# Whole-pair key loads in a cached-attention decode kernel, with three gathers on ScalarE and GpSimd and a later TensorE branch

## The chip, the core and the metric

The kernel runs on one core of a Trainium2 chip. The core has TensorE (matrix products; "PE" in the profile, with its weight loads as "PEld"), VectorE ("DVE"), ScalarE ("ACT"), GpSimd ("POOL") and SyncE ("SP"). Here SyncE only issues transfers, which run on the core's 16 DMA engines. The metric is the time of one execution in microseconds on the device, as the median of several runs.

## The reference

One token (`x` is 1x1x512) goes through a layer norm, attention over a cache of 16384 positions (8 key/value heads of width 128, four query heads on each) and a small mixer MLP. Cut to what matters:

```python
q = (ln(x) @ wq).reshape(1, 1, 32, 128)           # 32 query heads
p = softmax(q @ k.T * 128 ** -0.5)                # k_cache, v_cache: 8 x 16384 x 128, bf16
h = x + (p @ v).reshape(1, 1, 4096) @ wo          # wo: 4096 x 512
u = ln(h)
x1 = u + ...                                      # one position: the padded, shifted h is cut to zeros
out = h + x1 + gelu(ln(x1) @ w3) @ w4             # w3: 512 x 1792, w4: 1792 x 512
```

The token mixer shifts along a sequence of length one, so its shifted parts are zero and `w1`, `w2` are never read. What is read is 79 MB: the keys and values are 33.6 MB each, and `wq`, `wo`, `w3`, `w4` make the rest.

## The kernel before

The eight key/value heads are done as four pairs (`j` = 0 to 3). One pair's keys are 8 MB and its values are 8 MB. Each of the 128 partitions holds a contiguous run of 64 KB of either: `kb` takes a pair's keys (as two halves, `kb[0]` and `kb[1]`), `vb` a pair's values, and `kt` half a pair's transposed keys.

A small planner (`Program`) records every operation with the tiles it reads and writes, works out which operations must wait for which, and writes out each engine's program in the order of recording. An engine works its list strictly in order, so an operation that waits holds everything behind it on that engine. TensorE's part of the four pairs is written once as a loop over registers (`_tensor`), so the sequence of signals from VectorE must be alike in every pair. The operation with no function (`pe(None, ...)`, `dve(None)`) marks a place where a branch is put that never leads away, with a hint for the instruction fetch.

For each pair:

- VectorE transposes the keys (`transpose_keys`, L616) into `kt`, in doubles of two pieces (128x2048 words of 32 bits, two head positions in a word) or in single pieces (128x1024). A half is eight pieces. Pairs 0 to 2 use four doubles in each half; pair 3 uses two singles and three doubles in half 0 and eight singles in half 1.
- TensorE clears a score bank (L627) and adds four products per piece (L633), as soon as the piece is there. A piece of `kt` may be overwritten once TensorE has read it.
- When a half's transposes are done, SyncE issues the load of the next pair's same half (`load_keys(j + 1, y)`), 4 MB. Only the first pair is loaded as one transfer of 8 MB.
- The softmax runs on VectorE (L643 to L651), ScalarE (the exponential, L655) and VectorE again (L659). Meanwhile TensorE runs a spin of 14 passes of two products that nobody reads (L498).
- TensorE multiplies with the values (L670) once GpSimd has told that they have landed (L475) and `pt` is there. Then SyncE issues the next pair's values, since `vb` is free.
- `gather(j)`: VectorE adds four blocks of the result with a factor for each row (L687, L690, the tile `od`), TensorE sums over rows (L694), and VectorE scales and masks into `o_m` (L696).

Behind the pairs, `wo` is multiplied (L739, weights into the place of the keys' first half), then a layer norm, `w3` (L759), the gelu on ScalarE (L769, `hg`, two halves), its transposes on VectorE (L773, `hcol`), and `w4`: the first seven blocks as wide products (L782), copied out by VectorE into `osum` (L785), summed over rows by TensorE (L788), and the last seven blocks as 28 narrow products (L794). Two copies to `fin` (L799, L801) and the output's transfer (L802) end it. TensorE's branch stands between L782 and L788 and waits for the second half of `hcol`.

SyncE's list of transfers, all on one queue and in this order: `wq`, keys 0 (whole), values 0, keys 1 in halves, values 1, keys 2 in halves, values 2, keys 3 in halves, values 3, `wo` in two parts (behind half 0 of pair 3), `w3` and `w4` in three parts (behind half 1 of pair 3), the output.

Of the kernel before, what the change touches and what calls it, by code (L numbers as in the profile page):

```python
# [24 lines left out]
class Program:  # L25
# [150 lines left out]
    def _tensor(self):  # L176
# [51 lines left out]
        for o in loop:  # L228
            ds = [d for d in o.deps if d.own]
            assert not ds or o.at[0] == "value"  # L230
            assert not any(d.dma for d in o.deps)
            for d in ds:
                told.setdefault(o.at[1:3], set()).add((d.sem, d.val - d.worth + 1, d.val))
# [4 lines left out]
        assert v0 > 0 and first - step * last > 0  # L238

        r, rl, ry, rq, rk = (eng.alloc_register(n) for n in ("seen", "landed", "half", "query", "piece"))  # L240
        self.turn, self.turned = rk, KP * pieces
# [123 lines left out]
KP = 8 * DH  # L365
# [5 lines left out]
def bass_sequential_preLN__gqa_block_cached__mixer_s_mlp__decode_kernel(  # L371
# [13 lines left out]
    with ExitStack() as ctx:  # L385
# [60 lines left out]
        kb_all = sb("kb", [128, 256 * DH], BF16)  # L446
# [80 lines left out]
        def variance(i):  # L527
# [7 lines left out]
            for n in range(1 + i):  # L535
# [9 lines left out]
        load("k", kb_all[:, :], pair_rows(A_k_cache, 0), ("r", 0, 0),  # L545
             also=[("r", y, i) for y in range(2) for i in range(RPARTS) if y or i])
# [65 lines left out]
        def transpose_keys(y, cuts):  # L612
            for t, n in zip(cuts, [b - a for a, b in zip(cuts, [*cuts[1:], 8])]):
                view = lambda x, t=t, n=n: x[:, :].bitcast(I32).rearrange("p (x l w) -> p x (l w)", x=2, l=64)[
                    :, :, t * 512:(t + n) * 512]
                P.op("DVE", lambda e, view=view: e.transpose(view(kt), view(kb[y])),  # L616
                     r=[("r", y, i) for i in range(RPARTS)], w=[("kt", t + i) for i in range(n)], worth=n)

        def key_piece(at, n):
            part = kt[:, :].rearrange("p (x f) -> p x f", x=2)[:, :, bass.ds(at, KP)]  # L620
            return part.rearrange("p x (l b s e) -> p b e x l s", l=8, b=2, s=32, e=2)[:, n // 2, n % 2, :, :, :]
# [40 lines left out]
        def values(j):  # L662
            tiles = vb[:, :].rearrange("p (x c l d) -> p x l c d", x=4, c=8, l=8)
            for x in range(VP):
                P.part("value", j, x)
                for it in range(16 // VP):
                    for ct in range(4):
# [4 lines left out]
                            tiles[:, l // 8, l % 8, 4 * ch:4 * ch + 4, :], start=(l < 2), stop=(l >= 30)),  # L672
# [8 lines left out]
        def gather(j):  # L681

            O, key = O_ps[0], ("O", 0)
            for c in range(4):
                block = O[:, c * 128:(c + 1) * 128]
                if c == 0:
                    dve(lambda e, block=block: e.tensor_scalar(od[:, :], block, rowc[:, 0:1], None, ALU.mult),  # L687
                        r=[key, "rowc"], w=["od"], bank=[key])
                else:
                    dve(lambda e, block=block, c=c: e.scalar_tensor_tensor(  # L690
                        od[:, :], block, rowc[:, c:c + 1], od[:, :], ALU.mult, ALU.add),
                        r=[key, "rowc", "od"], w=["od"], bank=[key])
# [3 lines left out]
            dve(lambda e: e.scalar_tensor_tensor(  # L696
                o_m[32 * j:32 * j + 32, :, :], A_ps[0:32, 0:128].rearrange("p (d r) -> p d r", d=4), den[:, 0:1],
                maskdd[0:32, :].unsqueeze(2).to_broadcast([32, 4, 32]), ALU.mult, ALU.mult),
                r=["A", "den", "maskdd"], w=["o_m"], bank=["A"])
# [136 lines left out]
```

## Time and profile before

| what | us |
|---|---|
| median of three runs | 189.87 (189.81 to 189.93) |
| the profiled execution | 189.89 |
| its span, first to last instruction | 188.4 |

| engine | busy us | share of the span |
|---|---|---|
| PE | 137.8 | 73% |
| DVE | 115.8 | 61% |
| ACT | 9.3 | 5% |
| POOL | 5.9 | 3% |
| DMA engines (16, mean) | | 97.9% |

A row of a timeline has the start and the length of a group of instructions, the engine, the line of the kernel, the operation, the tile written and the tiles read, and how many there are; brackets hold the idle time before it and what ended it. A row of the chain of waits has start, length and what the time went to; for a transfer that is the time from its issue to its landing. A row by lines has the busy time, the mean of one in nanoseconds, and the idle time before. A row of transfers ends with the time from issue to landing.

### The profile page before, as it was taken

What the parts mean: (1) busy time and instruction counts of PE and PEld (TensorE: products, weight loads), DVE (VectorE), ACT (ScalarE), POOL (GpSimd) and SP (SyncE); (2) the same over time, 40 slices, a digit from 0 to 9 for tenths busy, and PEclk for the clock granted to TensorE, in tenths of its full rate; (3) what the DMA queues carried; (4) which work ended last, traced back from release to release, by engine and by line L of the source; (5) the groups of instructions that cost most, each with busy time, mean ns of one, the idle gap of its engine ahead of it and who ended that gap; (6) DMA issues with size and microseconds to landing.
All of it is one profiled execution on the core that took longest, in us unless ns stands there. A gap on an engine that the chain in (4) does not pass through costs nothing.

```text
span 188.4 us, 2532 instructions
## 1 busy us (share of the span) xinstructions
PE 137.8 (73%) x820; PEld 59.3 (31%) x824; DVE 115.8 (61%) x141; ACT 9.3 (5%) x16; POOL 5.9 (3%) x11
## 2 busy tenths in 40 slices
PE   1009700599989639998990999999319999886874
PEld 1004200234434413443450344345103433432332
DVE  4900741999645299994508999551449897513154
ACT  3000000000020000000200000020000000500011
POOL 1900000000000000000000000000000000000010
PEclk9999985569999975999998599999955999999998
DMA  6999999999799998999999999997999998899994
GB/s 223 445 445 445 445 445 445 445 445 445 334 445 445 445 543 362 417 389 403 445 445 445 445 445 445 445 445 334 445 445 445 556 403 362 362 440 450 397 411 183
DMA packets 2605, 79.19 MB, mean 420 GB/s; under 512 B 298, under 2 KB 300, under 8 KB 812
## 3 DMA queue, kind: packets, MB, share of 16 engines
q1 hardware_dynamic: 2596, 79.17, 97.9%
q8 instruction: 1, 0.02, 0.0%
q10 hardware_dynamic: 8, 0.00, 0.0%
HBM read 79.17 MB, written 0.00 MB: 420 GB/s over the span
## 4 chain that ended last, share of the span: by engine, by line
DMA 45%; PE 36%; DVE 16%; issue 2%; ACT 0%; SPq 0%; DVEq 0%
DMA kb<-in_A_k_cache_dram 32%; PE banks L633 22%; DMA kb<-in_B_w_dram 13%; DVE kt L616 12%; PE banks L498 6%; PE banks L670 4%; DVE mx L643 1%; PE banks L627 1%; DVE od L690 1%; PE banks L647 1%; PE banks L759 1%; PE banks L694 0%; DVE od L687 0%; DVE osum L785 0%; PE banks L782 0%
## 5 line engine op out<-in xcount | busy, mean ns | idle before, releaser
L616 DVE STREAM_TRANSPOSE kt<-kb 128x2048 int32<-128x2048 int32 (+1 forms) x37 | 71.0, 1985 | 10.4 <-DMA kb<-in_A_k_cache_dram 10.4
L633 PE MATMUL banks<-kt,qn 128*128 x256 | 69.1, 426 | 0.1
L633 PEld LDWEIGHTS banks<-kt,qn 128*128 x256 | 26.8, 105 | 41.0 <-issue 21.5
L498 PE MATMUL banks<-xn 128*128 128x512 bf16 x126 | 28.6, 381 | 0.0
L627 PE MATMUL banks<-qn 128*128 128x512 bf16 x8 | 3.9, 490 | 23.9 <-DVE kt L616 23.9
L498 PEld LDWEIGHTS banks<-xn 128*128 128x128 bf16 x130 | 12.7, 99 | 15.8 <-issue 2.4
L593 PE MATMUL banks<-vb,xn 128*128 x32 | 8.5, 432 | 9.7 <-DVE xn L584 9.7
L670 PE MATMUL banks<-vb,pt 128*32 128x512 bf16 x256 | 14.7, 379 | 0.7 <-POOLq L475 0.7
L659 DVE STREAM_TRANSPOSE pt<-p_sb 64x1024 bf16<-64x1024 bf16 x8 | 9.9, 1239 | 5.4 <-ACT p_sb L655 5.3
L655 ACT ACTIVATE p_sb<-banks,bias 128x1024 bf16<-128x1024 f32 x4 | 4.5, 1114 | 155.4 <-DVE nmh L651 155.4
L670 PEld LDWEIGHTS banks<-vb,pt 128*32 128x32 bf16 x256 | 8.7, 97 | 4.7 <-POOLq L475 0.8
L687 DVE TENSOR_SCALAR od<-banks,rowc 128x128 f32<-128x128 f32 x4 | 1.4, 351 | 14.2 <-PE banks L670 14.2
L643 DVE TENSOR_REDUCE mx<-banks 128x1 f32<-128x1024 f32 x4 | 4.9, 1224 | 8.1 <-PE banks L633 8.1
L627 PEld LDWEIGHTS banks<-qn 128*128 128x128 bf16 x8 | 0.8, 100 | 25.8 <-issue 25.4
L600 DVE STREAM_TRANSPOSE qcol<-banks 64x1024 f32<-64x1024 f32 x4 | 4.8, 1226 | 6.6 <-PE banks L593 6.6
L593 PEld LDWEIGHTS banks<-vb,xn 128*128 128x128 bf16 x32 | 3.5, 108 | 14.3 <-issue 11.6
L539 POOL TENSOR_TENSOR st<-st,expo 128x1 f32<-128x1 f32 (+1 forms) x2 | 1.3, 630 | 175.4 <-DVE st L537 175.4
L506 PE MATMUL banks<-mean 128*128 128x512 f32 (+1 forms) x12 | 6.5, 622 | 0.0
L694 PE MATMUL banks<-od,zo 128*32 128x128 f32 x8 | 1.6, 285 | 6.5 <-DVE od L690 6.5
L680 DVE RECIPROCAL den<-banks 32x1 f32<-32x1 f32 x4 | 0.6, 155 | 7.8 <-PE banks L678 7.8
L690 DVE SCALAR_TENSOR_TENSOR od<-banks,rowc,od 128x128 f32<-128x128 f32 x12 | 4.2, 351 | 0.4
L647 PE MATMUL banks<-mxd,mean 128*128 128x128 f32 x8 | 2.0, 326 | 2.4 <-DVE mxd L644 2.4
(81 smaller groups left out, 49.5 us busy)
## 6 DMA issues: line engine op xcount, KB each, us to landing
kb<-in_A_k_cache_dram SPq DMA_DIRECT2D x6, 4096.0 KB, 24.9
vb<-in_A_wq_dram SPq DMA_DIRECT2D x1, 4096.0 KB, 12.3
kb<-in_A_wo_dram SPq DMA_DIRECT2D x1, 3584.0 KB, 28.5
kb<-in_B_w_dram SPq DMA_DIRECT2D x1, 1792.0 KB, 24.2
kb<-in_B_w_dram SPq DMA_DIRECT2D x1, 896.0 KB, 26.0
kb<-in_B_w_dram SPq DMA_DIRECT2D x1, 640.0 KB, 27.1
kb<-in_A_wo_dram SPq DMA_DIRECT2D x1, 512.0 KB, 29.4
kb<-in_B_w_dram SPq DMA_DIRECT2D x1, 256.0 KB, 27.2
```

The source lines that it names most:

```text
L498: P.unread = lambda e: e.matmul(banks[:, 7, :], copies(xn[:, 0:1], 128), copies(xn[:, 0:1], 512), start=True, stop=True)
L506: pe(lambda e: e.matmul(banks[:, 7, 0:n], mean4[:, :], copies(mean4[:, 0:1], n), start=True, stop=True), r=["mean4"], w=["spare1"])
L593: pe(lambda e, k=k: e.matmul(row[:, bass.ds(P.b, 512)], copies(xn[:, k:k + 1], 128), wq_k[:, k, bass.ds(P.c, REP * DH)], start=(k == 0), s ...
L600: dve(lambda e, g=g, b=b, half=half: e.transpose(qcol[64 * g:64 * g + 64, 2 * b:2 * b + 2, :, :].rearrange("p e m u -> p (e m u)"), half.r ...
L616: P.op("DVE", lambda e, view=view: e.transpose(view(kt), view(kb[y])), r=[("r", y, i) for i in range(RPARTS)], w=[("kt", t + i) for i in r ...
L627: pe(lambda e: e.matmul(row[:, bass.ds(P.y, 512)], copies(none, 128), copies(none, 512), start=True, stop=False, skip_group_check=True), r ...
L633: pe(lambda e, n=n: e.matmul(row[:, bass.ds(P.y, 512)], qn[:, n, bass.ds(P.q, 128)], key_piece(P.k, n), start=False, stop=(n == 3), skip_g ...
L643: dve(lambda e: e.tensor_reduce(mx[:, :], s_all, AX.X, ALU.max), r=[("s", 0), ("s", 1)], w=["mx"], **both)
L655: act(lambda e: e.activation(p_sb[:, :], s_all, ACTF.Exp, bias=bias[:, 0:1], scale=float(SCALE), accum_out=acc[:, :]), r=[("s", 0), ("s", ...
L659: dve(lambda e, g=g: e.transpose(pt[64 * g:64 * g + 64, :, :, g, :], p_sb[64 * g:64 * g + 64, :]), r=["p"], w=["pt"])
L670: pe(lambda e, l=l, ct=ct, ch=ch: e.matmul(O_ps[0][32 * ct:32 * ct + 32, :], pt[:, l, ch, :, :].rearrange("p g u -> p (g u)"), tiles[:, l ...
L690: dve(lambda e, block=block, c=c: e.scalar_tensor_tensor(od[:, :], block, rowc[:, c:c + 1], od[:, :], ALU.mult, ALU.add), r=[key, "rowc", ...
```

## The change

Six things change.

1. Keys of pairs 1 and 2 are loaded as one transfer of 8 MB each. To let such a load start before the last transposes of the pair before it, the keys lie at shifting places in a longer `kb`: pair 0 four pieces up, pair 1 two pieces up, pairs 2 and 3 at the start. The last two pieces of pairs 0 and 1 then lie beyond what the next load writes. Pair 3 is still loaded in halves.
2. A piece of `kt` is contiguous (`KP` is 16 runs of 128 instead of two times 8), and the values are indexed to match.
3. Half 1 of every pair is transposed in eight single pieces.
4. The gathers of pairs 0 to 2 go to ScalarE (four scaled copies into `osum`, later the scaling into `o_m`) and GpSimd (two additions, later the mask). TensorE waits for GpSimd's signal. The gather of pair 3 stays on VectorE, with a GpSimd instruction that passes the signal on.
5. The spin of 14 passes is counted against VectorE's signals and grows from pair to pair, to 14 in the last.
6. TensorE's branch in the tail, and the 28 narrow products, wait for a ScalarE copy of the whole `hcol` (128x448) into `hg` instead of for `hcol` itself.

```diff
@@ _tensor: signals of the gather, and the spin
+            gs = [d for d in o.deps if d.own == "g"]
...
-                self._spin(eng, at[a])
+                passes, body = self.spins.get(id(at[a]), (0, 0))
+                if passes:
+                    by = step // 3
+                    assert now > by * passes
+                    eng.reg_mov(self.turn, now - by * passes)
+                    eng.br("pe_turn")
+                    nc.switch_bb("pe_turn", parent=None)
+                    for _ in range(body):
+                        self.unread(eng)
+                    eng.reg_add(self.turn, self.turn, by)
+                    eng.br_lt(self.turn, r, "pe_turn", "pe_turned")
...
+                if any(d.own == "g" for d in at[a].deps):
+                    eng.wait_ge(self.gathered, rl)
@@ sizes
-KP = 8 * DH
+KP = 16 * DH
+BASE = (4 * KP, 2 * KP, 0, 0)
...
-        kb_all = sb("kb", [128, 256 * DH], BF16)
+        kb_all = sb("kb", [128, BASE[0] + 256 * DH], BF16)
@@ loads of the keys
-        def load_keys(j, y):
+        def load_keys(j, y=None):
             n = 128 * DH
-            load(f"k{y}", kb[y][:, :], pair_rows(A_k_cache, j)[:, y * n:(y + 1) * n], ("r", y, 0),
-                 also=[("r", y, i) for i in range(1, RPARTS)])
+            if y is None:
+                load("k", kb_all[:, BASE[j]:BASE[j] + 2 * n], pair_rows(A_k_cache, j), ("r", 0, 0),
+                     also=[("r", y, i) for y in range(2) for i in range(RPARTS) if y or i] + [("tail", j)])
+            else:
+                load(f"k{y}", kb[y][:, :], pair_rows(A_k_cache, j)[:, y * n:(y + 1) * n], ("r", y, 0),
+                     also=[("r", y, i) for i in range(1, RPARTS)])
@@ transposes
+        def transpose_keys(j, y, cuts):
             for t, n in zip(cuts, [b - a for a, b in zip(cuts, [*cuts[1:], 8])]):
+                at = BASE[j] + (8 * y + t) * KP
+                apart = BASE[j] and y and t >= 6
+                P.op("DVE", lambda e, t=t, n=n, at=at: e.transpose(
+                    kt[:, t * KP:(t + n) * KP].bitcast(I32), kb_all[:, at:at + n * KP].bitcast(I32)),
+                     r=[("tail", j)] if apart else [("r", y, i) for i in range(RPARTS)],
+                     w=[("kt", t + i) for i in range(n)], worth=n)
@@ gather
+            if j < PAIRS - 1:
+                for c in range(4):
+                    act(lambda e, c=c: e.activation(osum[:, c * 128:(c + 1) * 128], O[:, c * 128:(c + 1) * 128],
+                                                    ACTF.Identity, scale=rowc[:, c:c + 1]),
+                        r=[key, "rowc"], w=[("osum", c)], bank=[key])
+                pool(lambda e: e.tensor_tensor(osum[:, 0:256], osum[:, 0:256], osum[:, 256:512], ALU.add),
+                     r=[("osum", c) for c in range(4)] + [("o_m", j - 1)], w=[("osum", 0), ("osum", 1)])
+                P.op("POOL", lambda e: e.tensor_tensor(od[:, :], osum[:, 0:128], osum[:, 128:256], ALU.add),
+                     r=[("osum", 0), ("osum", 1)], w=["od", "gathered"], own="g")
+            else:
...
+                P.op("POOL", lambda e: e.nop(), r=["od"], w=["gathered"], own="g")
             unread(1)
             pe(lambda e: e.matmul(A_ps[0:32, 0:128], zo[:, :], od[:, :], start=True, stop=True),
-               r=["od", "zo"], w=["A"], bank=["A"])
+               r=["gathered"], also=["od", "zo"], w=["A"], bank=["A"])
+            if j < PAIRS - 1:
+                act(lambda e: e.activation(to.rearrange("p d r -> p (d r)"), A_ps[0:32, 0:128], ACTF.Identity,
+                                           scale=den[:, 0:1]), r=["A", "den"], w=[("o_m", j)], bank=["A"])
+                pool(lambda e: e.tensor_tensor(
+                    to, to, maskdd[32 * j:32 * j + 32, :].unsqueeze(2).to_broadcast([32, 4, 32]), ALU.mult),
+                    r=[("o_m", j), "maskdd"], w=[("o_m", j)])
@@ the loop over the pairs
-                transpose_keys(y, (0, 2, 4, 6) if j < PAIRS - 1 else range(8) if y else (0, 1, 2, 4, 6))
+                transpose_keys(j, y, range(8) if y else (0, 2, 4, 6) if j < PAIRS - 1 else (0, 1, 2, 4, 6))
                 scores(j, y)
-                if j < PAIRS - 1:
+                if j == PAIRS - 2:
                     load_keys(j + 1, y)
+                elif j < PAIRS - 2 and y:
+                    load_keys(j + 1)
@@ the tail
-        pe(None, r=[("hcol", 1)])
+        act(lambda e: e.activation(hg[:, :], hcol[:, :, :].rearrange("p m u -> p (m u)"), ACTF.Identity),
+            r=[("hcol", 1)], w=["late", ("hg", 0), ("hg", 1)])
+        pe(None, r=["late"])
...
-                   r=[("hcol", 2 * m // NHC), ("r", 1, len(W3) + piece(W4, m))], w=["n"], bank=["mn"])
+                   r=["late", ("r", 1, len(W3) + piece(W4, m))], w=["n"], bank=["mn"])
```

More of the change, by code (lines that the diff above doesn't have):

```diff
@@ L228, in _tensor @@
         for o in loop:
-            ds = [d for d in o.deps if d.own]
+            ds = [d for d in o.deps if d.own == "v"]
+            gs = [d for d in o.deps if d.own == "g"]
             assert not ds or o.at[0] == "value"
+            assert not gs or o.at[0] in ("rest", "value")
             assert not any(d.dma for d in o.deps)
+            for d in gs:
+                assert d.val == o.at[1] + (o.at[0] == "rest")
+                self.gathered = d.sem
             for d in ds:
@@ L237, in _tensor @@
             assert lo_v <= v0 + parts * j + x <= hi_v
-        assert v0 > 0 and first - step * last > 0
+        assert v0 == 1 and first - step * last > 0
         r, rl, ry, rq, rk = (eng.alloc_register(n) for n in ("seen", "landed", "half", "query", "piece"))
-        self.turn, self.turned = rk, KP * pieces
+        self.turn, self.turned = rk, None
         hint = eng.mark_branch_hint_location()
```

50 lines of the change are left out of this document (24 added, 26 removed).

## The prediction

> **What bounds the kernel now.** I read the page first, then the chain of waits, then SyncE's timeline beside the times from issue to landing. From the page, the span, the DMA row of the 40 slices and the queues:
>
> ```profile
> span 188.4 us, 2532 instructions
> DMA  6999999999799998999999999997999998899994
> q1 hardware_dynamic: 2596, 79.17, 97.9%
> ```
>
> The 16 DMA engines work 97.9% of the span, and every slice but the first and the last reads 7 or more. From the chain of waits (start, length, what):
>
> ```profile
> 1.19 31.19 DMA kb<-in_A_k_cache_dram
> ...
> 119.03 29.68 DMA kb<-in_A_k_cache_dram
> ...
> 157.94 24.21 DMA kb<-in_B_w_dram
> ...
> 185.12 0.70 DVE osum L785
> ...
> 185.87 0.42 PE banks L788 x8
> ```
>
> The chain names compute in the middle, but its DMA pieces are times from issue to landing, most of which a transfer stands in line. Whether the line ever empties is seen from SyncE's timeline (start, length of the issue), and from the DMA view of short windows around single issues, in the order values 0, second key half of pair 1, values 1, second key half of pair 2, values 2, values 3 (last column: us from issue to landing):
>
> ```profile
> 22.43 0.33 SPq L463 DMA_DIRECT2D vb<-in_A_v_cache_dram  x1
> 41.44 9.05 SPq L463 DMA_DIRECT2D kb<-in_A_k_cache_dram  x2
> 64.38 0.33 SPq L463 DMA_DIRECT2D vb<-in_A_v_cache_dram  x1
> 75.78 9.10 SPq L463 DMA_DIRECT2D kb<-in_A_k_cache_dram  x2
> 98.73 0.33 SPq L463 DMA_DIRECT2D vb<-in_A_v_cache_dram  x1
> ...
> 133.21 0.33 SPq L463 DMA_DIRECT2D vb<-in_A_v_cache_dram  x1
> ...
> 187.29 0.33 SPq L802 DMA_DIRECT2D out_dram<-fin  x1
> ```
> ```profile
> vb<-in_A_v_cache_dram SPq DMA_DIRECT2D x1, 29.3
> ...
> kb<-in_A_k_cache_dram SPq DMA_DIRECT2D x1, 4096.0 KB, 21.0
> ...
> vb<-in_A_v_cache_dram SPq DMA_DIRECT2D x1, 26.1
> ...
> kb<-in_A_k_cache_dram SPq DMA_DIRECT2D x1, 4096.0 KB, 25.4
> ...
> vb<-in_A_v_cache_dram SPq DMA_DIRECT2D x1, 30.6
> ...
> vb<-in_A_v_cache_dram SPq DMA_DIRECT2D x1, 34.9
> ```
>
> Issue plus time to landing gives the landings (a second half is issued 0.33 before its "x2" group ends): keys 0 32.38, values 0 51.73, keys 1 50.16+21.0 = 71.16, values 1 90.48, keys 2 84.55+25.4 = 109.95, values 2 129.33, keys 3 148.71, values 3 168.11. The distances are 19.35, 19.43, 19.32, 19.47, 19.38, 19.38, 19.40 for 8 MB each: one unbroken stream, whatever the engines did meanwhile. The weights follow on (w3 lands at 157.94+24.21 = 182.15). So the end is set by bytes, by the count of transfers, and by the 6.2 us of tail behind w3. An edit that neither empties the line nor touches the tail is worth nothing.
>
> **The change part by part.** *Keys of pairs 1 and 2 in one transfer.* Two transfers fewer. Transfers sent whole (the values) average (19.35+19.32+19.38+19.40)/4 = 19.36; keys sent in halves (19.43+19.47+19.38)/3 = 19.43. A second transfer costs 0.07, so two pairs give -0.14. The rows' rounding (0.05) allows 0 to -0.3 for both.
>
> The price is that a key load now issues once instead of half by half. It waits for six of eight single transposes of the second half (pieces 6 and 7 lie beyond the region written, thanks to the shifted bases). VectorE's timeline for pair 0, and for the last half, which already runs in singles:
>
> ```profile
> 32.47 17.66 DVE L616 STREAM_TRANSPOSE kt<-kb 128x2048 int32<-128x2048 int32 x8 [6.46 <-DMA kb<-in_A_k_cache_dram]
> ...
> 148.74 9.13 DVE L616 STREAM_TRANSPOSE kt<-kb 128x1024 int32<-128x1024 int32 x8 [0.75 <-DMA kb<-in_A_k_cache_dram]
> 157.94 1.81 SPq L463 DMA_DIRECT2D kb<-in_B_w_dram  x4
> ```
>
> Half 0 is released at 41.44; six singles take 9.13×6/8 = 6.85, the hand-over 0.07: issue at 48.36, with values 0 landing at 51.73. The lead is 3.4 us (15.98 behind the keys' landing, against a transfer of 19.36), and the same in pair 1. What a cold issue needs is bounded by the output: issued at 187.29, over by 188.4, 1.1 us with its landing. Some 2.3 us are spare, so I cost this at nothing; the cover is the values in flight. Could TensorE hold the transposes up, since kt is overwritten while it is read? Its slowest half:
>
> ```profile
> 140.81 9.88 PE L633 MATMUL banks<-kt,qn 128*128 x32
> ```
>
> It begins about 2.4 after the landing (0.1 to start, 17.66/8 = 2.2 for a first double piece, 0.1 to hand over) and takes 9.88 for eight pieces at its slow start, so all are read 12.3 after the landing; VectorE overwrites the first at 9.0 and the last at about 17, each behind its reader. No stall. Pair 3 keeps its two half loads.
>
> *Three gathers on ScalarE and GpSimd, fewer passes of the spin, contiguous pieces, a GpSimd hop in the last gather.* The row of the spin's 28 matmuls, the only GpSimd row with two inputs, and TensorE's waits for values 3, wo and w3 in the last stretch:
>
> ```profile
> 161.04 6.29 PE L498 MATMUL banks<-xn 128*128 128x512 bf16 x28
> ```
> ```profile
> L539 POOL TENSOR_TENSOR st<-st,expo 128x1 f32<-128x1 f32 (+1 forms) x2 | 1.3, 630 | 175.4 <-DVE st L537 175.4
> ```
> ```profile
> PE banks L670 <- POOLq L475: 0.7, 1, 0.7
> ```
> ```profile
> 176.71 1.91 PE L739 MATMUL banks<-kb,o_b 128*32 128x512 bf16 x32 [0.17 <-DMA kb<-in_A_wo_dram]
> ...
> 182.29 0.94 PE L759 MATMUL banks<-kb,hc 128*32 128x448 bf16 x16 [0.34 <-DMA kb<-in_B_w_dram]
> ```
>
> VectorE is rid of five steps in each of three pairs, but its next transposes in pairs 1 and 2 now start when the whole 8 MB have landed (71.1 and 109.8), 6.7 and 11 us behind the old gathers' start at the values' end (64.38, 98.73). Nothing of it is gained there. With a third of a pair's VectorE count per pass, the spin runs 5, 8, 11 and 14 times instead of 14; at 6.29/14 = 0.45 a pass the early pairs save 4.0, 2.7 and 1.3. All it brings forward is the next values' issue, which stands in line anyway: pair 0's comes 32.0 behind its keys' landing, and 38.7 (two transfers) is when it is needed. The layout keeps its element counts. Nothing, then, for pairs 0 to 2; the hop in the last gather (a semaphore more) lies ahead of wo, for which TensorE waits. Queued behind the new work stand, on ScalarE, the next pair's exponentials and, on GpSimd, the word of the next values' landing (L475); both are wanted some 20 us later. On TensorE it is the next pair's scores, which only pair 3 can feel.
>
> There, its keys come in halves as before, VectorE is free for them at once, but TensorE must pass the gather of pair 2 first. Pair 2's values end at 109.8+32.0-1.3 (passes)-1.0 (the last single piece is shorter than a double) = 139.5. Four ScalarE steps at 0.3 (the rows of ScalarE below, less their overlap), two GpSimd additions at the 0.63 above and 0.5 for hand-overs and the small matmul make 3.1; 1.5 and 6 are bounds, from half and from three times the GpSimd row with ScalarE steps of 0.2 to 0.5. TensorE begins pair 3 at 142.6 rather than 140.4. A warm half of its scores, and the windows view of pair 3 (busy TensorE, granted clock, DMA):
>
> ```profile
> 79.34 7.39 PE L633 MATMUL banks<-kt,qn 128*128 x32
> ```
> ```profile
> 139.60:143.00 3.40, 2.58 (x7) 0.50 0.89 386
> 143.00:146.40 3.40, 3.40 (x10) 0.50 1.07 463
> 146.40:149.90 3.50, 3.50 (x18) 0.99 1.04 449
> ```
>
> Started at 142.6, with the clock at half until 146.4 again, it has two pieces by then (twice 7.39/8 = 1.85 each) and needs 6×7.39/8 = 5.5 for the others: 151.9, and 7.6 more for the second half: 159.5, against 158.9 now (its last keys' transposes plus one piece). That is 0.6 late. In front of the end stand waits of 0.7 for values 3, 0.17 for wo and 0.34 for w3, 1.2 in all, and 1.0 if the stream ends earlier. So nothing, with 0.4 to spare.
>
> *TensorE's branch behind a ScalarE copy of 128x448.* The rows of the second transpose that it waits for, of ScalarE's nearest widths, and of the wait that ends the tail:
>
> ```profile
> 183.80 1.05 DVE L773 STREAM_TRANSPOSE hcol<-hg 128x224 bf16<-128x224 bf16 x2 [0.68 <-ACT hg L769]
> ```
> ```profile
> L655 ACT ACTIVATE p_sb<-banks,bias 128x1024 bf16<-128x1024 f32 x4 | 4.5, 1114 | 155.4 <-DVE nmh L651 155.4
> ...
> L769 ACT ACTIVATE hg<-banks,st 128x224 bf16<-128x224 f32 x2 | 0.8, 488 | 1.7 <-PE banks L759 1.7
> ```
> ```profile
> PEld banks L794 <- DMA kb<-in_B_w_dram: 0.2, 1, 0.2
> ```
>
> A straight line between 224 wide (0.49) and 1024 (1.11) puts 448 at 0.66; I take that, with 0.49 and 1.11 as bounds. The copy starts at 184.85, ends at 185.5, and with 0.1 for semaphore and branch TensorE is free at 185.6. Behind it stand the four row-sum groups (L788) and the 28 matmuls of L794; they wait anyhow for VectorE's osum, over at 185.82, and start at 185.87. By the upper bound the start would be 186.06, 0.19 late, and the last eight have 0.2 of idle in front, ended by the last weights. So nothing, and 0.1 at worst. No shortening of the tail is in it either.
>
> The sum against the profiled execution's 189.89 (span 188.4 and 1.49 around it): -0.14, thus 189.75. The median shown is 0.02 below that execution, so 189.73 to compare with 189.87. A measurement of this kernel tells about 0.2% (0.38 us) from no change; this lies inside.
>
> **The rivals.** *Slower: the line runs dry ahead of keys 1 and 2.* It decides if the issue comes later than about 1.1 before the values' end, that is if fourteen pieces take 2.3 longer than the 15.98 counted. Each time the stream then stops, for 1.1 where the lead is zero: 189.73+2×1.1 = 191.9. For it: this is the only place where the change cuts a lead, from 10 us in the first half to 3.4. Against it: the transposes there show no wait inside a pair.
>
> *Slower: the tail's fetch of instructions.* The DMA view from 186 to 187 us, where the stream has ended:
>
> ```profile
> q8 instruction: 1, 0.02, 5.9%
> ```
>
> One packet of instructions takes 0.059×16 = 0.94 us, 1.2 or more behind the transposes that release the old branch. If TensorE needed its content, the row sums would start at 185.6+1.2+0.9 = 187.7 rather than 185.87: 189.73+1.8 = 191.5; if it only falls in the output's way, some 0.3, 190.0. Against it: the fetch starts behind 186.0, when TensorE is in its last matmuls, and TensorE's program keeps nearly its length. The Trainium skill's page "Runtime: NRT & Kernel Launch", section "Instruction fetch mechanics", says that fetching is sequential and that a taken branch outside the fetched blocks stalls for a fetch; this branch falls through, so by that rule the tail costs nothing more; the trace agrees (row sums 0.05 behind osum's end).
>
> *Slower: pair 3 begins too late.* It decides from a start behind about 143.0: then less than the window to 146.4 is busy, and the half clock may last one window longer. Four pieces at half speed to 149.9, four at 0.92, 153.6, and 7.6 more: 161.2, 2.3 late, 1.3 past the waits: 191.0. For it: the gather's cost is a guess from rows of other work. Against it: my middle is 0.4 on the good side. The Trainium skill, "TensorE: Matmul & The Clock Gate", Part 1, has the clock freed by one busy window of some 3.4 us; the trace agrees (0.50 to 146.4 after the first full window, 0.99 from there), and by it a start before 143.0 costs nothing.
>
> *No gain:* the 0.07 is not a cost per transfer, 189.87. *Faster by more:* the tail's fetch, now later, no longer meets the last weights and the last eight's 0.2 of idle goes too: 189.73-0.3 = 189.4.
>
> **How the numbers follow.** Forecast 0.43, no gain 0.23, late pair 3 0.13, dry line 0.06, fetch 0.05, faster by more 0.10. The first two are inside 0.2%: same 0.66; slower 0.24; faster 0.10. The likeliest one's own range is 189.6 to 189.9. For 8 in 10 it reaches to 189.45 below, and above to 190.5, which takes in the milder forms of a late pair 3 and of the fetch; their full prices and the dry line stay outside.
>
> **What would show it.** Keys 1 and 2 land about 19.35 behind the values before them, with no gap (right), or 20 and more (dry line). Their issues stand near 48.4 and 87. VectorE waits for keys in pairs 1 and 2, though free. TensorE takes up pair 3 between 142 and 143, and its scores end near 159.5. The ScalarE copy takes 0.5 to 0.8 and the row sums still start within 0.1 of osum's end. w3 lands near 182.0. The prediction is wrong if the stream's end moves by more than 0.3, or if the tail behind it changes by as much.

## The result and the profile after

The kernel after takes 190.97 us in the median of six runs (190.68 to 191.13), the kernel before 189.88 beside it (189.81 to 190.13). The ratio is 1.0054, with a 95% interval of 1.0044 to 1.0064: slower by 1.0 to 1.1 us, where the prediction had 189.73 and a range up to 190.5. The profiled execution of the kernel after took 191.13.

The page of the kernel after, with the span, the DMA row of the 40 slices and the queue:

```profile
span 189.7 us, 2447 instructions
DMA  6999999999999999999898999999999999989992
q1 hardware_dynamic: 2308, 79.17, 97.3%
```

As before, no slice inside reads under 8, and the share falls only from 97.9% to 97.3%. By this view alone the stream looks as unbroken as it was. The chain of waits of the kernel after (start, length, what) says where to look:

```profile
1.19 31.14 DMA kb<-in_A_k_cache_dram
...
48.15 24.04 DMA kb<-in_A_k_cache_dram
...
88.01 22.87 DMA kb<-in_A_k_cache_dram
...
119.94 20.00 DMA kb<-in_A_k_cache_dram
...
162.02 1.24 DVE mx L668
...
164.11 6.12 PE banks L522 x28
...
186.60 0.70 DVE osum L831
...
187.35 0.43 PE banks L836 x8
```

Keys 1 are issued at 48.15 and landed at 48.15+24.04 = 72.19; before it was 71.16. Keys 2 landed at 88.01+22.87 = 110.88 (109.95). And from 139.95 on the chain no longer runs through the weights' transfer but through pair 3's scores, the spin and the values: computing sets the end.

A transfer's landing is one number in such rows, that of its last engine. The trace also has the moment at which each of the 16 DMA engines reports its part. First and last of the sixteen, in us from the start of the span:

| transfer | before | after |
|---|---|---|
| keys 0 | 31.83–32.38 | 31.78–32.33 |
| values 0 | 51.19–51.73 | 51.13–51.69 |
| keys 1 | 70.62–71.16 | 70.78–72.19 |
| values 1 | 89.99–90.51 | 90.13–91.53 |
| keys 2 | 109.48–109.94 | 109.54–110.88 |
| values 3 | 167.69–168.06 | 167.66–169.00 |
| w3 | 181.77–182.15 | 181.73–183.11 |

The first engine is on time to the end (181.73 against 181.77), and fourteen of the sixteen have landed keys 1 by 71.39. The last one falls behind by 1.0 at keys 1 and never catches up, since it has work in line all the time: 0.96 late with w3. A load counts as landed when the last engine has reported, so the whole kernel goes by the slowest of sixteen, while the mean share hardly moves.

The second loss is in pair 3. Timeline of the kernel after, from the gather of pair 2 to the end of pair 3's scores:

```profile
141.50 1.14 ACT L711 ACTIVATE osum<-banks,rowc 128x128 f32<-128x128 f32 x4 [6.66 <-PE banks L695]
...
142.72 0.73 POOL L714 TENSOR_TENSOR osum<-osum 128x256 f32<-128x256 f32 x1 [36.42 <-ACT osum L711]
143.53 0.46 POOL L716 TENSOR_TENSOR od<-osum 128x128 f32<-128x128 f32 x1
...
144.03 0.41 PE L730 MATMUL banks<-od,zo 128*32 128x128 f32 x2 [2.27 <-POOL od L716]
...
144.60 0.39 PE L652 MATMUL banks<-qn 128*128 128x512 bf16 x1 [0.16 <-DVE kt L639]
...
144.93 8.25 PE L658 MATMUL banks<-kt,qn 128*128 x32
145.99 0.56 PEld L658 LDWEIGHTS banks<-kt,qn 128*128 x4 [0.51 <-issue]
...
153.72 8.26 PE L658 MATMUL banks<-kt,qn 128*128 x32
...
162.02 1.23 DVE L668 TENSOR_REDUCE mx<-banks 128x1 f32<-128x1024 f32 x1 [3.22 <-PE banks L658]
```

The gather takes 141.45 to 144.55, 3.1 us as I had it. But it starts 1.95 later than I had it, TensorE takes up pair 3 at 144.6 instead of 142.6, each piece of the scores takes 8.25/8 = 1.03, and the scores end at 162.0 instead of 159.5 (before: 159.1). The clock is not to blame: in the view of windows the stretch that had 0.50 before now reads 1.00 in the column of the granted clock (behind the length and the busy times of the five engines stand the granted clock, the DMA share and GB/s).

```profile
143.00:146.40 3.40, 2.18 (x9) 0.90 (x10) 3.40 (x2) 0.36 (x1) 1.30 (x3) 1.00 1.05 453
```

Last, the tail of the kernel after: the new copy and what follows it.

```profile
186.39 0.58 ACT L832 ACTIVATE hg<-hcol 128x448 bf16<-128x448 bf16 x1 [0.75 <-DVE hcol L819]
186.60 0.69 DVE L831 COPY osum<-banks 128x512 f32<-128x512 f32 x1 [0.25 <-PE banks L828]
187.35 0.16 PEld L836 LDWEIGHTS banks<-osum,row 128*32 128x32 f32 x8 [1.29 <-DVE osum L831]
187.35 0.43 PE L836 MATMUL banks<-osum,row 128*32 128x128 f32 x8 [0.79 <-DVE osum L831]
```

The copy is over at 186.97, osum at 187.29, and the row sums start 0.06 behind osum, as before.

### The profile page after: what moved, and what is told of

The parts are those of the page before. It is cut to its first block, busy times and chain, and to the rows that moved or that the text cites. A ratio compares the mean times of both kernels' runs of the same rounds, so it can differ in the third digit from the quotient of the medians.

```text
span 189.7 us, 2447 instructions
## 1 busy us (share of the span) xinstructions
PE 129.5 (68%) x788; PEld 54.3 (29%) x788; DVE 111.6 (59%) x138; ACT 14.4 (8%) x32; POOL 10.6 (6%) x20
## 3 DMA queue, kind: packets, MB, share of 16 engines
q1 hardware_dynamic: 2308, 79.17, 97.3%
## 4 chain that ended last, share of the span: by engine, by line
DMA 52%; DVE 27%; PE 19%; issue 1%; ACT 0%; SPq 0%; DVEq 0%; POOLq 0%
DMA kb<-in_A_k_cache_dram 52%; DVE kt L639 24%; PE banks L658 9%; PE banks L522 5%; PE banks L695 2%; PE banks L785 1%; DVE mx L668 1%; DVE od L725 1%; PE banks L530 1%; PE banks L805 0%; PE banks L652 0%; DVE osum L831 0%; DVE osum L789 0%; PE banks L828 0%; DVE hcol L819 0%
## 5 line engine op out<-in xcount | busy, mean ns | idle before, releaser
L639 DVE STREAM_TRANSPOSE kt<-kb 128x1024 int32<-128x1024 int32 (+1 forms) x49 | 71.8, 1534 | 32.7 <-DMA kb<-in_A_k_cache_dram 32.7
L658 PE MATMUL banks<-kt,qn 128*128 x256 | 67.4, 411 | 0.1
L658 PEld LDWEIGHTS banks<-kt,qn 128*128 x256 | 26.1, 102 | 39.8 <-issue 21.4
L522 PE MATMUL banks<-xn 128*128 128x512 bf16 x94 | 22.2, 381 | 0.0
L522 PEld LDWEIGHTS banks<-xn 128*128 128x128 bf16 x94 | 9.1, 99 | 11.5 <-issue 2.6
L695 PEld LDWEIGHTS banks<-vb,pt 128*32 128x32 bf16 x256 | 8.2, 97 | 4.5
L714 POOL TENSOR_TENSOR osum<-osum 128x256 f32<-128x256 f32 x3 | 2.2, 724 | 127.9 <-ACT osum L711 127.9
L711 ACT ACTIVATE osum<-banks,rowc 128x128 f32<-128x128 f32 x12 | 3.4, 368 | 19.4 <-PE banks L695 19.4
L604 DVE COPY zo<-rowgh 128x32 f32<-128x32 f32 x1 | 3.6, 3632 | 0.0
```

Source lines behind the costliest of these rows:

```text
L522: P.unread = lambda e: e.matmul(banks[:, 7, :], copies(xn[:, 0:1], 128), copies(xn[:, 0:1], 512), start=True, stop=True)
L604: dve(lambda e, z=z, m=m: e.tensor_copy(z[:, :].rearrange("p (n d) -> p n d", d=4), m[:, :, :].rearrange("p g h -> p (g h)").unsqueeze(2). ...
L639: P.op("DVE", lambda e, t=t, n=n, at=at: e.transpose(kt[:, t * KP:(t + n) * KP].bitcast(I32), kb_all[:, at:at + n * KP].bitcast(I32)), r=[ ...
L658: pe(lambda e, n=n: e.matmul(row[:, bass.ds(P.y, 512)], qn[:, n, bass.ds(P.q, 128)], key_piece(P.k, n), start=False, stop=(n == 3), skip_g ...
L695: pe(lambda e, l=l, ct=ct, ch=ch: e.matmul(O_ps[0][32 * ct:32 * ct + 32, :], pt[:, l, ch, :, :].rearrange("p g u -> p (g u)"), tiles[:, l ...
```

## The experiments

Theory to begin with: the whole load of keys 1, issued 3.5 us ahead of the values' landing, makes some DMA engines lose time. Rivals: the gathers on ScalarE and GpSimd, the tail's copy, the late computing of pair 3. Every ratio is to the kernel before, measured again beside the run (medians 189.76 to 189.89).

**Keys 1 and 2 in halves again, all else as in the kernel after.**

```diff
-BASE = (4 * KP, 2 * KP, 0, 0)
+BASE = (0, 0, 0, 0)
...
-                if j == PAIRS - 2:
+                if j < PAIRS - 1:
                     load_keys(j + 1, y)
-                elif j < PAIRS - 2 and y:
-                    load_keys(j + 1)
```

> The changed kernel with the keys of pairs 1 and 2 again loaded in two halves, each issued behind its half's transposes (no shifted bases). Theory A (a key load issued only 3.4 us ahead lets some DMA engines fall behind at the hand-over, and they never catch up): keys 1 land at 71.2 instead of 72.2, the sixteen landings of each transfer again lie within 0.6 us instead of 1.4, w3 lands at 182.2. Theory B (the computing chain of pairs 2 and 3 is late by itself, whatever the transfers do): pair 2 also starts earlier here, since its first half lands at 100.2, so TensorE takes up pair 3 by 141 and its scores end near 159. Both give about 189.9 us; a rival that puts the loss into the tail or into the new gather gives 190.7 or more.

Measured: 189.76 us, ratio to before 0.9999 (0.999 to 1.0007). Its chain of waits:

```profile
50.29 20.77 DMA kb<-in_A_k_cache_dram
...
80.28 29.56 DMA kb<-in_A_k_cache_dram
...
119.07 29.55 DMA kb<-in_A_k_cache_dram
...
157.84 24.22 DMA kb<-in_B_w_dram
```

Keys 1 land at 71.06, w3 at 182.06, and the weights end the chain again. So the loss comes with the whole loads and the time at which they are issued; the two are separated below. The gathers, the passes of the spin, the contiguous pieces, the singles and the copy in the tail together cost nothing that can be measured (0.2 us at most), with the keys in halves.

**The copy in the tail taken out** (TensorE's branch and the narrow products wait for `hcol` again; the rest as after).

```diff
-        act(lambda e: e.activation(hg[:, :], hcol[:, :, :].rearrange("p m u -> p (m u)"), ACTF.Identity),
-            r=[("hcol", 1)], w=["late", ("hg", 0), ("hg", 1)])
-        pe(None, r=["late"])
+        pe(None, r=[("hcol", 1)])
```

> The changed kernel without the ScalarE copy: TensorE's branch and the narrow products wait for the transposed gelu as before. As predicted (the copy ends before osum does): within 0.1 us of the changed kernel. The rival (the copy or the later fetch is on the path): faster by 0.2 us or more.

Measured: 190.84, ratio 1.0056 (1.0044 to 1.0068), like the kernel after. The copy costs nothing and saves nothing that these intervals, some 0.2 us to either side, can show.

**A shorter spin in the softmax**, ten passes for fourteen in the last pair, so that computing ends some 1.8 us earlier (four passes at 0.45).

```diff
-            P.spin(14)
+            P.spin(10)
```

> The changed kernel with the spin 4 passes (1.8 us) shorter in every pair; only in pair 3 does TensorE wait for it. If the computing chain behind pair 3 alone sets the end: its values start 1.1 us earlier (169.0, their landing) and the time falls by 1.1 to 1.2 to 189.8 us. If the lagging DMA engine stands right behind it: the last eight products then wait for the last weights at 187.5, and the time falls by 0.3 to 0.4 only, to 190.65 us.

Measured: 190.85 (190.31 to 191.93), ratio 1.0071 (1.0051 to 1.0091); the profiled execution took 190.31. In it the chain of waits goes by the transfers to the end:

```profile
48.14 23.69 DMA kb<-in_A_k_cache_dram
...
158.51 24.19 DMA kb<-in_B_w_dram
```

Keys 1 land at 71.83 here, w3 at 182.70. So behind the late computing stands the late engine: in this execution, with the computing out of the way, the end goes by that engine. Its lag differs from one profiled kernel to the next with the same place of issue (keys 1 at 71.83 here, 72.19 in the kernel after). That the other executions here, up to 191.93, are longer for a larger lag is likely, but not shown: only one was profiled.

**The first load earlier, the second later.** The bases let keys 1 issue after twelve pieces and keys 2 after all sixteen.

```diff
-BASE = (4 * KP, 2 * KP, 0, 0)
+BASE = (4 * KP, 0, 0, 0)
...
-                apart = BASE[j] and y and t >= 6
+                apart = BASE[j] and y and t >= 4
```

> The changed kernel with bases 4, 0, 0, 0 pieces instead of 4, 2, 0, 0: keys 1 may be issued four pieces before the end of pair 0's transposes (lead 5.7 us), keys 2 only behind the last piece of pair 1 (lead about 1 us). Theory A: no lag at keys 1 (landing 71.1, spread 0.6 us), and a lag of 1 us or more on most engines at keys 2 (landing 111 or later); time 191 to 191.8 us. The rival, a hiccup that belongs to the first whole-pair load whatever its lead: keys 1 still land at 72.2 with a spread of 1.4.

Measured: 191.17, ratio 1.0075 (1.0062 to 1.0088). Chain of waits:

```profile
45.96 25.15 DMA kb<-in_A_k_cache_dram
...
89.18 21.87 DMA kb<-in_A_k_cache_dram
```

Keys 1, issued 5.8 ahead of the values' landing (51.76), land at 71.11: nothing lost. Keys 2, issued 1.3 ahead of values 1 (90.45), land at 111.05, and now all sixteen engines are late (110.44 to 111.05, against 109.48 to 109.94). In these two loads the loss goes with the lead; the runs below show that it does not always do so.

**Keys 2 alone whole, issued early.** For this and the runs below, a list says which pairs load whole, and halves go to the shifted places too.

```diff
-BASE = (4 * KP, 2 * KP, 0, 0)
+BASE = (4 * KP, 4 * KP, 0, 0)
+WHOLE = (2,)
...
-                apart = BASE[j] and y and t >= 6
+                apart = j + 1 in WHOLE and y and t >= 8 - (BASE[j] - BASE[j + 1]) // KP
...
-                if j == PAIRS - 2:
+                if j < PAIRS - 1 and j + 1 not in WHOLE:
                     load_keys(j + 1, y)
-                elif j < PAIRS - 2 and y:
+                elif j < PAIRS - 1 and y:
                     load_keys(j + 1)
```

> The changed kernel with keys 1 in two halves again and only keys 2 whole, issued four pieces before the end of pair 1's transposes (bases 4, 4, 0, 0; lead about 5.7 us), so that no DMA engine should fall behind (w3 at 182.1, the sixteen landings of a transfer within 0.6 us). Theory A alone (the lag of the DMA engines is all of the loss): 189.75 us, as before. Theory B (a whole load of keys 2 makes pair 2 start at 109.8 and end too late for pair 3, whatever the DMA engines do): TensorE takes up pair 3 at about 143.5, its scores end near 160.8, and the time is 190.5 to 190.8 us.

Measured: 190.04, ratio 1.0007 (0.9998 to 1.0016). Keys 2 are issued at 75.64 and land at 109.62 on the last engine; w3 at 181.83: no lag. The lead is 14.6 us and not the 5.7 expected: with keys 1 in halves, VectorE starts on pair 1 when the first half is there. So in the kernel after keys 2 are late also because keys 1 are whole. TensorE's rows of pair 3 in the timeline:

```profile
143.34 0.61 PE L654 MATMUL banks<-qn 128*128 128x512 bf16 x1 [0.16 <-DVE kt L641]
...
143.74 8.48 PE L660 MATMUL banks<-kt,qn 128*128 x32
...
152.44 8.27 PE L660 MATMUL banks<-kt,qn 128*128 x32
```

The scores end at 160.7, 1.6 later than before, with no transfer late. The chain of waits is in computing at the end, but the time is only 0.15 us above that before (interval -0.04 to 0.3). With the shorter spin as well:

```diff
-            P.spin(14)
+            P.spin(10)
```

> The kernel of e6 with the spin 4 passes (1.8 us) shorter. If in e6 the computing chain behind pair 3 sets the end, this takes it back off the path: 189.65 to 189.8 us, bound by the transfers. If e6 is bound by the transfers, no difference from e6.

Measured: 189.70, ratio 0.9992 (0.9983 to 1.0001). So a late pair 3 by itself is worth about 190.04-189.70 = 0.34 us, and the lag must carry the rest of the loss.

**Both loads whole, with other leads.** The first one's edit; the second has `3 * KP` in the place of `1 * KP`.

```diff
-BASE = (4 * KP, 4 * KP, 0, 0)
-WHOLE = (2,)
+BASE = (4 * KP, 1 * KP, 0, 0)
+WHOLE = (1, 2)
```

> The changed kernel with bases 4, 1, 0, 0: keys 1 issued three pieces before the end of pair 0's transposes (lead about 4.5 us) and keys 2 one piece before the end of pair 1's (about 2.3 us). Theory A by lead alone: keys 1 land at 71.1 to 71.3 without a lag, keys 2 lag by 0.5 us or more on most engines. If the hand-over ahead of keys 1 is special and the second one forgives a short lead (in the changed kernel keys 2 lost nothing at 2.1 to 3.5 us): no lag at either.

> The changed kernel with bases 4, 3, 0, 0: keys 1 issued one piece before the end of pair 0's transposes (lead about 2.3 us), keys 2 three pieces (about 4.5 us). Theory A: keys 1 lag by more than the 1.1 us of the changed kernel on the slowest engine, or on more of the engines; keys 2 add nothing. Time 191 us or more.

Measured: 190.40 (189.97 to 192.42), ratio 1.0059 (1.0028 to 1.0091), in two groups, 189.97 to 190.54 and 191.75 to 192.42; and 190.12, ratio 1.0012 (1.0003 to 1.0021). The profiled execution of the first, from the lower group, lost nothing at keys 1 (lead 4.7) and 0.1 at keys 2 (issued 88.11, 2.4 ahead); no execution of the upper group was profiled, so what it lost there is not known. In the second, keys 1 were issued at 49.44, with a lead of 2.4, less than in the kernel after, and landed at 71.19 without a loss; keys 2, with a lead of 4.7, lost 0.1. "The shorter the lead, the more is lost" did not hold, nor did the 191 us or more expected of the second. As two loads at two leads mix, the next runs leave pair 2 in halves.

**Keys 1 alone whole, the lead scanned.** The base of pair 1 goes from 0 to 4 pieces, and the load issues after twelve to sixteen of pair 0's sixteen pieces. The edit for fourteen:

```diff
-BASE = (4 * KP, 4 * KP, 0, 0)
-WHOLE = (2,)
+BASE = (4 * KP, 2 * KP, 0, 0)
+WHOLE = (1,)
```

> The kernel after, with the keys of pair 1 alone in one transfer (pair 2 in halves), and its bases such that the load can issue after twelve pieces instead of fourteen, some 5.8 us before the values land instead of 3.4. Theory (the short hand-over is the cause, not the whole load): no engine lags, keys 1 land at 71.1 on all sixteen, 189.6 to 189.9. Rival (a transfer of 8 MB that follows another is itself slower on some engines): keys 1 spread to 71.9 or 72.2, 190.4 to 191.0.

> Keys 1 whole after thirteen pieces (twelve gave 189.72, fourteen 190.63), pair 2 in halves; the load issues near 47.1, 4.1 to 4.6 ahead of the values' landing. Theory (there is a lead from which nothing is lost, between 3.4 and 5.8, and the loss grows as it gets shorter): 189.7 to 190.3. Rival (a sharp bound near 3.4): 189.75.

> As the one before, but with the bases of the change for pair 1, so that the load of keys 1 issues after fourteen pieces, near 48.15, 3.4 us before the values land. It is the change with pair 2's keys in halves. Theory (all that is lost is lost at the hand-over ahead of keys 1): the last engine lands keys 1 0.8 to 1.1 late, w3 and w4 as late, 190.4 to 190.8, a little less than the 190.97 of the change, since the start of pair 3 has less to wait for. Rival (it takes both late loads, the one of pair 2 too): 189.8.

> Keys 1 whole after fifteen pieces, pair 2 in halves; the load issues near 49.3, 1.8 to 2.4 ahead of the landing. Theory (the loss grows with a shorter lead): 190.7 to 191.3. Rival (only a distance of 3.0 to 3.5 meets the engines badly; an earlier run with such a lead had no lag in its profile): 189.75 to 190.1.

> Keys 1 whole after all sixteen pieces, pair 2 in halves; the load issues near 50.4, 0.7 to 1.3 ahead of the landing. Both theories: all engines wait, by about 1.2 as a run with such a lead ahead of keys 2 showed, 190.8 to 191.3; with the bound of the prediction (an issue needs 1.1) it would be 189.8 to 190.2.

The rows of the chain of waits with the load of keys 1 after twelve, thirteen, fourteen, fifteen and sixteen pieces, one kernel each:

```profile
45.94 25.12 DMA kb<-in_A_k_cache_dram
```
```profile
47.01 24.01 DMA kb<-in_A_k_cache_dram
```
```profile
48.13 23.97 DMA kb<-in_A_k_cache_dram
```
```profile
49.39 21.95 DMA kb<-in_A_k_cache_dram
```
```profile
50.48 21.93 DMA kb<-in_A_k_cache_dram
```

The lead is the landing of values 0 on the last engine less the issue. The last two columns come from the records of single packets: the sixteen first 64 KB packets of keys 1, one for each engine, how long they took, and the idle time of an engine before its own. The records do not name the engine, so a packet is put behind one that had just ended; where that can be done in two ways, the table has both ends.

| pieces | lead | keys 1 landed | time | ratio (95%) | first packets took: least, middle, most | longest idle before |
|---|---|---|---|---|---|---|
| 12 | 5.8 | 71.06 | 189.72 | 0.9993 (0.9985–1.0002) | 2.42, 2.42, 2.42 | 0.0 |
| 13 | 4.7 | 71.02 | 189.72 | 0.9989 (0.998–0.9998) | 2.42, 2.42, 2.42 | 0.0 |
| 14 | 3.5 | 72.10 | 190.63 | 1.0046 (1.0029–1.0063) | 2.53, 2.7, 3.18 | 0.7 to 0.8 |
| 15 | 2.4 | 71.34 | 189.90 | 1.0001 (0.9991–1.001) | 2.42, 2.7, 3.16 | 0.0 |
| 16 | 1.3 | 72.41 | 191.06 | 1.006 (1.0047–1.0073) | 2.42, 2.8, 3.43 | 1.3 to 2.0 |

Twelve against fourteen pieces is the same kernel but for one base: 0.9 us for 2.2 us less lead. With 4.7 or more every first packet takes exactly what all others take. With 3.5 and less most engines' first packet is longer (12 to 16 of the sixteen), and with 1.3 the engines also stand still first. That fifteen pieces cost less than fourteen was no accident of one run (two kernels; keys 1 land 19.35 and 19.54 behind values 0, where they take 19.43 before): the first packets are as slow, but no engine stands idle, and the slow ones are not those that come last: the three engines that start at 51.38 to 51.44 take 2.42 to 2.51. Why is open.

The lead alone does not decide. In the kernel after, in the one without the copy and in the one with the shorter spin, keys 2 are issued whole with a lead of 3.5 as well, 2.1 to 2.6 ahead of the first engine's landing. They land 19.35 to 19.36 behind values 1, without a loss. Their first packets take 2.42 in the last two, and 2.52 to 2.66 on five engines in the first. So the runs show that at keys 1 the issue after fourteen pieces loses time and the one after thirteen does not. They do not show a lead that is enough, or too short, everywhere.

**Two transfers of 4 MB at the late place.** Is it the length of the transfer? In the first try both halves' loads write all of the keys' tiles:

```diff
-                    load_keys(j + 1)
+                    load_keys(j + 1, 0)
+                    load_keys(j + 1, 1)
...
-                     also=[("r", y, i) for i in range(1, RPARTS)] + [("tail", j)] * y)
+                     also=[("r", y, i) for i in range(1, RPARTS)] + [("r", 1, i) for i in range(RPARTS)] * (j == 1 and not y) + [("tail", j)] * y)
```

> As the one before with the load of keys 1 at the same late place, but as two transfers of 4 MB one right behind the other. Theory (the time of issue is what counts): the same lag, keys 1 to 71.9 or later on the last engine, 190.4 to 190.8. Rival (one long transfer hands its first packets out more slowly than a short one): no lag, 189.8.

Measured: 192.92, ratio 1.0159 (1.0143 to 1.0175). SyncE's timeline of this kernel:

```profile
48.13 14.68 SPq L484 DMA_DIRECT2D kb<-in_A_k_cache_dram  x2
```

The second issue stands at 48.13+14.68-0.33 = 62.48, behind the landing of the first at 62.46. So it doesn't answer the question, but it prices a line that runs dry: the engines end the first half's packets at 60.8 to 62.1 and begin the second's at 63.5 to 64.3, and keys 1 land at 74.48, 3.3 late (71.16 before). With both issued at once:

```diff
+                    P.op("SP", lambda e: e.nop(), w=[("r", y, i) for y in range(2) for i in range(RPARTS)])
+                    load_keys(j + 1, 0)
+                    load_keys(j + 1, 1)
-                    load_keys(j + 1)
```

> The run before this with two halves held the second one back until the first had landed. Here both are issued at once: keys 1 as two transfers of 4 MB, one right behind the other, after fourteen pieces, near 48.2. Theory (the time of issue counts, not the length): the last engine lands keys 1 at 71.7 or later, 190.4 to 190.8. Rival (the long transfer hands out its first packets more slowly): no engine lags, 189.7 to 189.9.

Measured: 190.91, ratio 1.0053 (1.0041 to 1.0066); keys 1 land at 71.94 on the last engine and at 70.83 on the first. Two transfers at the late place lose as one does, so it is not the length that costs; it is the place of the issue.

**Later by empty instructions on SyncE**, twelve of them ahead of the load after fourteen pieces.

```diff
+                    for _ in range(12):
+                        P.op("SP", lambda e: e.nop(), r=[("r", 1, i) for i in range(RPARTS)])
                     load_keys(j + 1)
```

> As the one with the late whole load of keys 1, with twelve empty instructions on SyncE ahead of the load, so that it issues some 0.6 to 1.2 us later yet (2.2 to 2.8 ahead of the values' landing). Theory (the shorter the lead, the more engines run dry): all engines lag, by 0.5 to 1.2, 190.6 to 191.2. Rival (only a certain distance, 3.0 to 3.5 ahead of the last packet, meets the engines badly, as the run with the load at 49.44 had no lag): keys 1 by 71.3, 189.8 to 190.1.

Measured: 190.80, ratio 1.004 (1.0024 to 1.0056). The instructions did not wait for the transposes, so the issue moved by 0.17 only, to 48.30; it is a second sample of the same lead, with the same lag (keys 1 at 72.15).

## Why the prediction was wrong, step by step

- **Two transfers fewer, -0.14:** not contradicted, not shown. The runs without a lag or a late pair 3, one transfer fewer each, stand at 0.9992, 0.9993 and 0.9989, with one interval just clear of 1.
- **The lead:** the mechanism and its size were right. 3.4 us predicted, 51.69-48.15 = 3.54 measured.
- **The step that failed** is "What a cold issue needs is bounded by the output [...] 1.1 us with its landing. Some 2.3 us are spare, so I cost this at nothing". The bound was too low: with the load after sixteen pieces, the engines' first packets of keys 1 began 0.95 to 2.24 us behind the issue at 50.48; the output is a transfer of 1 KB and no measure for that. And a packet that starts in time is not yet a packet that costs nothing: in the kernel after no engine stood idle for more than 0.3 us ahead of keys 1, yet their first packets took up to 3.57 us for 2.42. Instead of nothing, the late issue of keys 1 costs 0.8 to 1.1 us; issued one or two pieces sooner, at leads of 4.7 and 5.8, it costs nothing, and one piece later, at 2.4, nothing that the time shows (1.0001). Why the packets are slow stays open.
- **My rival of the dry line** was the nearest: same place, twice 1.1 for a lead of zero. Its condition (less than 1.1 ahead) was as wrong as the step. That the time can be lost on one engine of sixteen, with no slice of the DMA row showing it, was in none of my cases. At keys 2, issued 3.5 ahead of the last engine's landing but 2.1 ahead of the first's, nothing more was lost: the spread that keys 1 left stayed at 1.3 to 1.4.
- **TensorE at pair 3:** 142.6 predicted, 144.6 measured, 2.0 late. 1.1 are the landing of keys 2 (110.88 for 109.8); 0.85 lie in pair 2 between that landing and the end of its values (30.57 for 29.7). There I had taken off 1.0 because the last single piece is shorter than a double, and that gain did not come. The operation behind the scores (pair 0 before, then pair 2 after) starts 52.31-32.38 = 19.93 and 130.79-110.88 = 19.91 behind the keys. VectorE's last piece was done 1.9 us ahead of that (110.98+17.91 = 128.89), so TensorE's own pace set the end of the scores. The gather's 3.1 was right.

```profile
52.31 1.12 PE L506 MATMUL banks<-mean 128*128 128x512 f32 x2
```
```profile
130.79 1.12 PE L530 MATMUL banks<-mean 128*128 128x512 f32 x2
```

- **The scores of pair 3:** I priced a warm piece at 7.39/8 = 0.92, from a half that follows one begun at half clock. There the weight loads of the first five pieces run without a gap (the row below, from the kernel before). In pair 3 of the kernel after, at full clock from the start, a piece takes 1.03, with 0.44 to 0.51 of "issue" before each later piece's weight loads, although VectorE was ahead (half 0 all transposed by 148.92). What fills the "issue" time is not shown. My scores took 16.9 and 17.4 were measured, but that is near by luck: I had counted half clock until 146.4, which did not come (1.00 there), so my first half took 9.3 for 8.8 measured, and my second 7.6 for 8.6.

```profile
79.13 4.22 PEld L633 LDWEIGHTS banks<-kt,qn 128*128 x20
```

- **What that cost:** I had 0.4 to spare in front of the end. The scores end 2.9 later than before, the stream 0.96, so the cover was gone and computing took over the end, as the rival of a late pair 3 had it, though from lateness and not from the half clock. Where the lag is taken away and computing stays late by 1.6, 0.15 us is left, inside the noise.
- **Right:** the stream as what sets the end of the kernel before, and of the versions without a lag or a late pair 3; no stall of the transposes; VectorE waiting for keys in pairs 1 and 2; no gain and no cost of the gathers for pairs 0 to 2; the copy (0.66 predicted, 0.58 measured), row sums 0.06 behind osum; no row of the tail waits for the instruction fetch.

## What to carry to other kernels

When a stream of transfers sets the end, a later issue of one of them must be checked by its lead over the landing of the transfer ahead of it, and the bound for that lead must come from a transfer of the same kind in a busy queue, not from a small one at the end. Even then it is worth measuring each place, since the same lead of 3.5 us cost up to 1.1 us at keys 1 and nothing at keys 2. Read the landings of all sixteen engines, not the mean share: an engine that loses a microsecond in a line that never empties keeps it to the end, and the kernel goes by the slowest. The cheap repair here is a base that lets the load go one piece earlier: keys 1 whole after thirteen pieces and pair 2 in halves takes 189.72, with the best ratio to before of all versions, though by 0.1% only.

## What the runs showed of the hardware

- At keys 1 an issue 3.5 us ahead of the landing before it slows the first packet on nearly all engines (from 2.42 to as much as 3.57 us); at 4.7 and 5.8 it slows none. At keys 2 the same 3.5 slows none in two profiles and five of sixteen in a third (2.66 at most). The Trainium skill's page "DMA: Bandwidth & Descriptors", section "Anatomy of one DMA — SWDGE (gpsimd) path", puts most of a fixed 2 us on completion and calls the setup small. That is told for transfers that GpSimd issues, and no run here shows that split; on SyncE's queue, with the load after sixteen pieces, 0.95 to 2.24 us passed from the issue to the engines' first packets, and that delay reached the time.
- The loss does not grow evenly with a shorter lead: keys 1 land 1.0 late at 3.5, -0.1 and 0.1 at 2.4 (two kernels), 1.2 at 1.3 (against 19.43 behind the values). The runs show that it is so, not why.
- A second transfer of 4 MB in a busy queue costs next to nothing (19.43 for a pair's keys in two halves against 19.36 for its values in one). The Trainium skill's page "SBUF — State Buffer", section "The DMA setup-cost knee (why "@ 1 MiB" ≠ asymptote)", advises the largest single transfer since each pays about 2 us; here a whole load in place of two halves gained at most 0.1 to 0.2 us where the issue was early, and lost 0.8 to 1.1 where it was late, as two halves issued together at that late place did too.
